# Moving second weight roundings, one output bank and one set of query loads in a thresholded attention with a squared-ReLU layer

## The chip, the cores and the metric

The kernel runs on one core of a Trainium2 chip. The metric is the device time of one execution in microseconds (us); lower is better. The core's engines work side by side, each through its own list of instructions in order: TensorE (PE) multiplies matrices, VectorE (DVE), ScalarE (ACT) and GpSimd (POOL) work on elements, and SyncE (SP) issues transfers. POOL and ACT issue transfers as well.

## The reference

For 8 batches of 8 heads with 576 rows of 64 numbers, attention whose scores below the row's maximum less `tau` are left out, then a layer with a squared ReLU over all 4608 rows:

```python
scores = np.matmul(q, k.transpose(0, 1, 3, 2)) / np.sqrt(64)
scores = np.where(scores >= max(scores, axis=-1) - tau, scores, -1e9)
attn = exp(scores - max(scores)); attn = attn / (sum(attn) + 1e-9)
x = np.matmul(attn, v)            # (B,H,S,D), turned to 4608 x 512
h = np.maximum(x @ w_in, 0.0)     # 512 x 2048
out = (h * h) @ w_out             # 2048 x 512
```

## The kernel before, in words

**Visits and steps.** Two heads of a batch are a pair; a pair is worked on in a visit `n`. A visit has steps `s`, one for each block `i` of 128 query rows; block 4 holds the last 64 rows of both heads. The first four pairs are visited twice: visits 0-3 take blocks 0 and 1 (steps 0-7), visits 4-7 blocks 2, 3, 4 (steps 8-19). Visits 8-11 take five blocks each (steps 20-39); from visit 12 on (step 40) visits go in twos, whose last 64 query rows share one step, the first of the two visits. The order of the work is written out by hand: a loop over the steps hands each engine its instructions in program order, and the engines wait for each other by semaphores alone.

**One step.** PE computes the scores into two banks (`scores`, L247); DVE takes the row maximum (L269); ACT computes the exponents (`exponents`, L277-280); DVE masks and sums (`threshold`, L292-295). There is one pair of score banks, so the next step's scores wait for the mask. POOL divides by the sum (`divide`, L300-302), for one tile of 576 columns in a step of block 4 before visit 12 and for two tiles otherwise. Two steps later PE turns the weights around (`turn`, L326-338), ACT copies them out (L327-339), and `mix` (L428) multiplies them with the values; ACT puts the result into `xT` (L411). From step 35 on (`first_dma`, visit 11) the turning is done by DVE in blocks of 32 (L366) and by transfers that SP issues (L378-391), and `mix` runs once a visit. In the last step of visits 4 to 10, DVE also turns the next visit's queries and keys (`prep`, L226) between the maximum and the mask.

**Weight roundings.** The two weight matrices come in 32 pieces `p` of 512 KB as 64-bit numbers. SP loads each into one of three areas (`load_weights`, L125), and `round_weights` rounds it in five stages: 0 two ACT copies (L137, L138), 1 and 2 three DVE operations (L140, L141, L144), 3 and 4 one POOL operation each (L146, L148). `pieces[s]` says how many are rounded in a step: one in steps 2, 4 and 6 and in each step from 8 on, but two in steps 24 and 29, up to step 34. The first of a step goes through its stages beside the step's own work. A second one gets all its stages at the step's end; on DVE that is still behind the mask and ahead of the next maximum. The end of a rounding lets SP load piece `p + 3`.

**The layer.** Rows go through the layer in chunks `j` of 256. Chunk 0 is done plainly (`j < PLAIN`): 16 calls of `mlp_in` (L476; ACT's relu L486, POOL's square L487), then 16 of `mlp_out` (L510), each of which adds the share of one of the 16 blocks of hidden units to two output banks; then ACT copies both banks to `osb` (L517) and POOL issues the store (L523). Later chunks have 16 of `mlp_in` and 14 half `product`s (L543), which read sums `gsum` that POOL makes (L466, L467) and sums of weights that DVE makes (L500). Below, each such call is a piece of the layer. `fill` hands pieces out four times in a step at a pace that `rate` sets from what is left, but only when enough roundings are done: an entry of `waiting` names the number it needs, and `usable` is the number done at the end of the step before last. Which step gets which piece is therefore fixed when the program is built. `next_bank` gives banks in turn, from 6 and 7 alone up to step 37. The plain layer's output banks are 7 for the first 128 rows and 6 for the others; the first piece of chunk 1 takes bank 6.

**Loads.** From visit 11 on queries, keys and values go into the list `loads`, which POOL works off with `some_loads`: one transfer a call, four calls a step, two a call when more than eight are in the list. `q_left` holds the last 64 query rows for a pair of visits (`load_left`, eight transfers of 8 KB, L190); DVE turns it into `qmid` (`prep_left`, L230). For visit 12 the loads are listed in step 37 behind four key loads and ahead of four query loads, and turned in step 39.

Of the kernel before, what the change touches and what calls it, by code (L numbers as in the profile page):

```python
# [19 lines left out]
def kernel(  # L20
# [10 lines left out]
    nc = tc.nc  # L31
# [3 lines left out]
    P = 128  # L35
    HP = H // 2
    NPAIR = B * HP
    NBLK = S // P
# [3 lines left out]
    NFT = d_ff // P  # L42
    TCH = 2 * P
    NCH = n_tokens // TCH
    HF, HD = NFT // 2, d_model // 2
# [17 lines left out]
    wo = const.tile([P, 7, HF, HD], FP32, name="wo")  # L63
    Q00, Q10, Q11, Q01 = range(4)
# [22 lines left out]
    q_left = const.tile([P, 2, REST // 32, 32], FP32, name="q_left")  # L87
# [68 lines left out]
    def rows_32(t, n, m):  # L156

        b, h = divmod(visits[n][0], HP)
        return t[b, 2 * h + m // 2, :, (m % 2) * 32:(m % 2) * 32 + 32].rearrange("(c p) d -> p c d", p=32)
# [21 lines left out]
    def load_left(n):  # L181

        for m in range(4):
            for v_ in range(2):
                loads.append((q_left[m * 32:(m + 1) * 32, v_, :, :], rows_32(q, n + v_, m)[:, NBLK * P // 32:, :]))

    def some_loads():
        for _ in range(min(1 + (len(loads) > 8), len(loads))):
# [85 lines left out]
    def exponents(vis, i):  # L274
        w, sc, st = weights[vis, i]
        mx, thr, bias = (st[:, j, 0:len(sc)] for j in range(3))
        nc.scalar.activation(out=bias, in_=mx, func=AF.Copy, scale=-SCALE)  # L277
        nc.scalar.activation(out=thr, in_=mx, func=AF.Identity, bias=ntau8)  # L278
        for u in range(len(sc)):
            nc.scalar.activation(out=w[:, u, :].rearrange("p (h k) -> p h k", h=2), in_=sc[u][:, :, 0:HALF],  # L280
                                 func=AF.Exp, bias=bias[:, u:u + 1], scale=SCALE)
# [220 lines left out]

    def mlp_out(j, f):

        if f == 0:
            used["o"] = [take("mm", (6, 7)) for t in range(2)]
        o = used["o"]
        for t in range(2):
            mov = wo[:, Q00:Q01 + 1:Q01 - Q00, f, :] if f < HF else wo[:, Q10:Q11 + 1, f - HF, :]
            nc.tensor.matmul(o[t].rearrange("p (h d) -> p h d", h=2), g[:, f, t * P:(t + 1) * P], mov,  # L510
                             start=(f == 0), stop=(f == NFT - 1))
        if f < NFT - 1:
            return []

        def store():
            for t in range(2):
                nc.scalar.copy(osb[:, t, :], o[t])  # L517
            store_rows(j, 0, 2)
        return [store]

    def store_rows(j, t0, t1):
        lo = j * TCH
        nc.gpsimd.dma_start(out=out[lo + t0 * P:lo + t1 * P, :].rearrange("(t p) d -> p t d", p=P), in_=osb[:, t0:t1, :])  # L523
# [57 lines left out]
    def paired(n):  # L581

        return n >= 3 * HP
# [45 lines left out]
    def pieces_of(j):  # L629

        todo = [((x // 4 + 1) * NMC, mlp_in, j, x) for x in range(NFT)]
        if j < PLAIN:
            todo += [(n_in + f + 1, mlp_out, j, f) for f in range(NFT)]
        else:
            todo += [(n_pieces, product, j, x, half) for x in range(len(PRODUCTS)) for half in range(2)]
        return todo
# [43 lines left out]
    for s, (n, i) in enumerate(steps):  # L680
        if s < HP * FIRST:
            x = int(n > 0 and i == 0)
        else:
            x = 2 if n >= 2 * HP and i == NBLK else 1
        pieces.append(min(x, left))
        left -= pieces[-1]
    assert left == 0
# [3 lines left out]
    def end_rounding(p):  # L691
        round_weights(p, 4)
        state["rounded"] += 1
        if p + RAW < n_pieces:
            load_weights(p + RAW)
# [3 lines left out]
    for s, (n, i) in enumerate(steps):  # L699
        if not by_dma(n) or i != visits[n][1][0] or paired(n) and n % 2:  # L700
            continue
        nxt = n + (2 if paired(n) else 1)
        more = nxt < len(visits)
        if paired(n):

            place_at[s + (2 if paired(n - 1) else 3)].append((n, 2, (0, 1)))
            place_at[s + 3] += [(n, 2, (2, 3)), (n, 0)]
            place_at[s + 5].append((n, 1))
            place_at[s + 8].append((n + 1, 0))
            place_at[s + 9].append((n + 1, 1))  # L710
            prep_at[s].append(lambda n=n: prep_part(q, n))
            load_at[s].append(lambda n=n: load_part(q, n + 1))
            load_at[s + 2].append(lambda n=n: load_v(n))
            prep_at[s + 4].append(lambda n=n: prep_part(q, n + 1))
            load_at[s + 4].append(lambda n=n: load_v(n + 1))
        else:
            place_at[s + 3].append((n, 0))
            place_at[s + 4].append((n, 1))
            place_at[s + 5].append((n, 2))
        if more:  # L720
            a, b, c, d = (s + 1, s + 5, s + 7, s + 8) if paired(n) else (s + 1, s + 2, s + 4, s + 4)
            load_at[a].append(lambda n=nxt: load_part(k, n))
            if paired(n):
                load_at[a].append(lambda n=nxt: load_left(n))
            prep_at[b].append(lambda n=nxt: prep_part(k, n))
            load_at[b].append(lambda n=nxt: load_part(k, n + 1))
            if not paired(n):
                load_at[b].append(lambda n=nxt: load_left(n))
            load_at[b].append(lambda n=nxt: load_part(q, n))
            prep_at[c].append(prep_left)  # L730
            prep_at[d].append(lambda n=nxt: prep_part(k, n + 1))
# [9 lines left out]
    for s in range(END + 1):  # L741
        state["step"] = s
        state["usable"] = rounded_by[-1]
        rounded_by.append(state["rounded"])
        on = s < NST
        now = []
        if on:
            n, i = steps[s]
            at = visits[n][1].index(i)
            last = at == len(visits[n][1]) - 1  # L750
            now = list(range(done, done + pieces[s]))
            done += pieces[s]
            more = n + 1 < len(visits)
            short = n < 2 * HP
            if short and at == 0 and 0 < n + 1 < 2 * HP:
                load_qk(n + 2)
            elif not short and at == 1 and not by_dma(n):
                load_qk(n + 1)
            if now:
                round_weights(now[0], 0)  # L760
            scores(s)
        old = steps[s - 2] if 2 <= s < NST + 2 and not by_dma(steps[s - 2][0]) else None
        at_once = now or old or early()
        lay = on and last and more and not by_dma(n)
        if old:
            turn(*old, 0)
            turn(*old, 1)
        if on:
            exponents(n, i)
            if at == 1:  # L770
                split_left(n)
            if lay:
                prep(n + 1)
            elif now:
                round_weights(now[0], 1)
        if s in mixes and not old:
            mix(*mixes[s])
            for j in chunk_at.get(s, ()):
                add_chunk(j)
        quarter = rate(s) / 4 if s < END else 1e9  # L780
        fill(quarter)
        if s in mixes and old:
            mix(*mixes[s])
            for j in chunk_at.get(s, ()):
                add_chunk(j)
        if old:
            turn(*old, 2)
        state["free"] = s > first_dma
        if on:
            threshold(n, i)  # L790
            for fn in prep_at[s] + load_at[s]:
                fn()
            if lay and now:
                round_weights(now[0], 1)
            if now:
                round_weights(now[0], 2)
                round_weights(now[0], 3)
            if not at_once:
                divide(n, i)
        if 0 < s <= NST and by_dma(steps[s - 1][0]):  # L800
            m, x = steps[s - 1]
            turn_blocks(m, x)
        for what in place_at[s]:
            place_blocks(*what)
        some_loads()
        fill(quarter)
        some_loads()
        if on and at_once:
            divide(n, i)
        fill(quarter)  # L810
        some_loads()
        fill(quarter)
        some_loads()
        if on:
            if now:
                end_rounding(now[0])
            for p in now[1:]:
                for stage in range(4):
                    round_weights(p, stage)
                end_rounding(p)  # L820
            if at == 0 and 0 < n <= 2 * HP:
                load_v(n)
            elif last and n >= 2 * HP and not by_dma(n):
                load_v(n + 1)
# [35 lines left out]
```

## Time and profile before

| what | value |
|---|---|
| time, median of 16 runs | 1414.88 us (1411.89 to 1416.31) |
| the profiled execution | 1415.92 us, span of its instructions 1414.1 us |
| mean granted TensorE clock | 0.989 |
| busy: PE, DVE, ACT, POOL | 1364.5, 855.7, 440.1, 922.1 us |
| eight matmuls of a layer piece, `xT` by `w_in` | 1.73 us |
| eight scores matmuls of a step | 1.17 to 1.24 us |
| one row maximum (L269), one mask (L292) | 0.75, 0.81 us |
| L140, L141, L144 at their shortest | 0.42, 0.69, 0.41 us |
| L146 and L148 on POOL | about 1.27 us each |
| POOL's issue of a `q_left` load; issue to landing | 0.55; 2.0 us |

A row of the profile names an engine, the line of the kernel, the operation, and what it writes and reads. A wait is an idle time of an engine, put down to what ended it. Times of a stretch count from the first instruction. The steps below are cut where DVE starts a step's first row maximum: step 16 at 102.5 us, 24 at 155.2, 29 at 190.6, 34 at 226.5, 37 at 255.1, 41 at 295.8.

### The profile page before, as it was taken

What the parts mean: (1) busy time and instruction counts of PE and PEld (TensorE: products, weight loads), DVE (VectorE), ACT (ScalarE), POOL (GpSimd) and SP (SyncE); (2) the same over time, 40 slices, a digit from 0 to 9 for tenths busy, and PEclk for the clock granted to TensorE, in tenths of its full rate; (3) what the DMA queues carried; (4) which work ended last, traced back from release to release, by engine and by line L of the source; (5) the groups of instructions that cost most, each with busy time, mean ns of one, the idle gap of its engine ahead of it and who ended that gap; (6) DMA issues with size and microseconds to landing.
All of it is one profiled execution on the core that took longest, in us unless ns stands there. A gap on an engine that the chain in (4) does not pass through costs nothing.

```text
span 1414.1 us, 22712 instructions
## 1 busy us (share of the span) xinstructions
PE 1364.5 (96%) x7556; PEld 1044.3 (74%) x7556; DVE 855.7 (61%) x1898; ACT 440.1 (31%) x1068; POOL 922.1 (65%) x1239
## 2 busy tenths in 40 slices
PE   5898988999999999999999999999999999999998
PEld 3676655767777777777777877777777777788887
DVE  5888887676767676766666666656666666501011
ACT  3776655222232223222222222222223222210110
POOL 3687878767777777777776858585868665422332
PEclk9999999999999999999999999999999999999999
DMA  7664531236555555554545555454445544310000
GB/s 151 133 143 107 134 99 46 51 68 130 99 116 99 114 95 110 95 107 89 104 83 112 105 109 93 100 90 96 93 103 95 120 83 95 63 42 16 1 16 15
DMA packets 397605, 127.95 MB, mean 90 GB/s; under 512 B 379952, under 2 KB 386288, under 8 KB 397488
## 3 DMA queue, kind: packets, MB, share of 16 engines
q1 hardware_dynamic: 373936, 93.01, 35.0%
q0 software_dynamic: 21168, 33.19, 8.9%
q8 instruction: 61, 1.00, 0.3%
q10 hardware_dynamic: 2384, 0.30, 0.1%
q14 instruction: 56, 0.46, 0.1%
HBM read 50.59 MB, written 9.44 MB: 42 GB/s over the span
## 4 chain that ended last, share of the span: by engine, by line
PE 87%; DVE 4%; ACT 3%; POOL 2%; issue 2%; DMA 1%; SPq 1%; POOLq 0%; ACTq 0%; DVEq 0%
PE bank L476 34%; PE bank L543 28%; PE s L247 12%; PE bank L428 10%; PE bank L326 1%; PE bank L510 1%; DVE turned L141 1%; DVE st L269 1%; ACT w L280 1%; ACT wT L327 1%; DVE w L292 1%; POOL g L487 1%; POOL w L302 0%; DVE turned L140 0%; POOL gsum L466 0%
## 5 line engine op out<-in xcount | busy, mean ns | idle before, releaser
L476 PE MATMUL bank<-xT,w_in_sb 128*128 128x256 f32 x2304 | 521.3, 384 | 2.1 <-ACT osb L517 2.1
L476 PEld LDWEIGHTS bank<-xT,w_in_sb 128*128 128x128 f32 x2304 | 433.6, 191 | 83.3 <-issue 22.3
L269 DVE TENSOR_REDUCE st<-s 128x1 f32<-128x576 f32 x288 | 205.8, 752 | 234.8 <-PE s L247 234.6
L292 DVE SCALAR_TENSOR_TENSOR w<-s,st,w 128x576 f32<-128x576 f32 x269 | 209.2, 814 | 112.3 <-ACT w L280 112.1
L543 PE MATMUL bank<-wo,gsum 128*128 128x256 f32 x1088 | 252.6, 384 | 6.1 <-POOL gsum L466 6.0
L302 POOL TENSOR_SCALAR w<-w,st 128x576 f32<-128x576 f32 x269 | 224.4, 843 | 24.8 <-DVE st L295 18.3
L543 PEld LDWEIGHTS bank<-wo,gsum 128*128 128x128 f32 x1088 | 204.0, 190 | 48.9 <-issue 12.5
L487 POOL TENSOR_TENSOR g<-g 128x512 f32<-128x512 f32 x144 | 152.0, 1056 | 114.3 <-ACT g L486 113.0
L277 ACT ACTIVATE st<-st 128x2 f32<-128x2 f32 (+1 forms) x148 | 30.3, 205 | 599.1 <-DVE st L269 598.6
L247 PE MATMUL s<-kT,qT 64*128 64x288 f32 x1024 | 175.7, 439 | 30.0 <-DVE w L292 14.8
L543 PE MATMUL bank<-wo,g 128*128 128x256 f32 x816 | 187.5, 382 | 0.0
L280 ACT ACTIVATE w<-s,st 128x576 f32<-128x576 f32 x269 | 183.3, 732 | 0.4 <-ACT st L278 0.2
L366 DVE STREAM_TRANSPOSE turned<-w 128x512 f32<-128x512 f32 (+2 forms) x388 | 168.8, 489 | 13.5 <-DMA wT<-turned 12.7
L543 PEld LDWEIGHTS bank<-wo,g 128*128 128x128 f32 x816 | 153.4, 190 | 28.4 <-issue 6.4
L428 PE MATMUL bank<-wT,vs 128*64 128x128 f32 (+7 forms) x1700 | 169.6, 359 | 3.0 <-ACT wT L327 2.6
L300 POOL TENSOR_SCALAR st<-st 128x2 f32<-128x2 f32 (+1 forms) x148 | 34.4, 232 | 207.8 <-DVE w L292 197.5
L247 PEld LDWEIGHTS s<-kT,qT 64*128 64x128 f32 x1024 | 99.1, 190 | 90.1 <-issue 61.4
L428 PEld LDWEIGHTS bank<-wT,vs 128*64 128x64 f32 (+1 forms) x1700 | 97.0, 138 | 77.3 <-issue 26.1
L486 ACT ACTIVATE g<-bank 128x512 f32<-128x512 f32 x144 | 86.1, 600 | 176.9 <-PE bank L476 175.9
L190 POOL DMA_DIRECT2D vs<-in_v_dram x144 | 90.6, 634 | 0.0
L557 DVE TENSOR_TENSOR gsum<-g 128x512 f32<-128x512 f32 x34 | 22.9, 702 | 110.6 <-PE bank L543 110.6
L146 POOL TENSOR_TENSOR turned<-turned 128x512 f32<-128x512 f32 x32 | 41.1, 1284 | 46.0 <-DVE turned L144 42.8
(73 smaller groups left out, 1049.7 us busy)
## 6 DMA issues: line engine op xcount, KB each, us to landing
wT<-turned SPq DMA_DIRECT2D x800, 72.0 KB, 2.3
out_dram<-osb POOLq DMA_DIRECT2D x34, 256.0 KB, 2.8
wo<-in_moe_w_in_dram SPq DMA_DIRECT2D x16, 512.0 KB, 4.6
wo<-in_moe_w_out_dram SPq DMA_DIRECT2D x16, 512.0 KB, 3.8
kl<-in_k_dram POOLq DMA_DIRECT2D x100, 72.0 KB, 3.1
ql<-in_q_dram POOLq DMA_DIRECT2D x100, 72.0 KB, 2.8
wT<-turned SPq DMA_DIRECT2D x192, 36.0 KB, 2.3
vs<-in_v_dram POOLq DMA_DIRECT2D x50, 128.0 KB, 3.2
```

Source lines behind the costliest of these rows:

```text
L190: nc.gpsimd.dma_start(out=to, in_=src)
L247: nc.tensor.matmul(sc[u][to, half, 0:HALF], lhsT, keys[rows, half * HALF:(half + 1) * HALF], start=True, stop=True)
L269: nc.vector.tensor_reduce(out=mx[:, u:u + 1], in_=sc[u][:, :, 0:HALF], axis=AX.XY, op=ALU.max)
L280: nc.scalar.activation(out=w[:, u, :].rearrange("p (h k) -> p h k", h=2), in_=sc[u][:, :, 0:HALF], func=AF.Exp, bias=bias[:, u:u + 1], sca ...
L292: nc.vector.scalar_tensor_tensor(out=wu, in0=sc[u][:, :, 0:HALF], scalar=thr[:, u:u + 1], in1=wu, op0=ALU.is_ge, op1=ALU.mult, accum_out=s ...
L302: nc.gpsimd.tensor_scalar(out=w[:, u, :], in0=w[:, u, :], scalar1=z[:, u:u + 1], scalar2=rcp[:, u:u + 1], op0=ALU.add, op1=ALU.mult)
L366: nc.vector.transpose(wb[:, at:at + k1 - k0, i % 2, :], w[:, u, k0 * 32:k1 * 32].rearrange("p (k q) -> p k q", q=32))
L428: nc.tensor.matmul(ps[u * D:(u + 1) * D, :], vs[n % 2][rows, u * (NBLK + 1) + c, :], wT[rows, NBLK if c == NBLK else u * (NBLK + 1) + c, a ...
L476: nc.tensor.matmul(h[:, x % 2, :], w_in_sb[:, c, f * P:(f + 1) * P], xT[:, c, at:at + TCH], start=(c == 0), stop=(c == NMC - 1))
L486: nc.scalar.activation(out=to, in_=h, func=AF.Relu)
L487: nc.gpsimd.tensor_tensor(out=to, in0=to, in1=to, op=ALU.mult)
L543: nc.tensor.matmul(to, left[:, f, :], wo[:, slot, f, :], start=(f == 0), stop=(f == HF - 1))
```

## The change

It has four parts.

1. The steps with two roundings are others. Before they were steps 24 and 29; now they are 16, 19 and 24 (block 4 of visits 6, 7 and 8). The last piece is rounded in step 33 instead of 34, and one step later than that its successors in the layer may start.
2. A second rounding's stage 0 now stands right behind the step's exponents, and stages 1 to 3 right behind the first piece's stages 2 and 3, behind the mask; only stage 4 stays at the step's end. On POOL both operations L146 so stand ahead of the step's division.
3. In the plain layer's output the last two calls change: call 14 adds blocks 14 and 15 to the first bank (7), call 15 adds both to the second (6). Each bank is copied by its own `store`; both rows are stored after the second. Call 14 now needs all 32 roundings.
4. `q_left` for visit 12 is loaded in step 27 by SP, directly, instead of in step 37 by way of `loads` and POOL.

By the planner's own working the pieces of the layer move with the gates: steps 14 to 43 had 1, 2, 1, 0, 2, 2, 0, 0, 3, 1, 1, 2, 1, 2, 1, 1, 1, 2, 1, 1, 1, 1, 5, 4, 4, 4, 4, 4, 4, 1 pieces and have 2, 1, 1, 0, 2, 2, 0, 3, 1, 1, 2, 1, 2, 1, 2, 1, 1, 1, 1, 1, 0, 5, 4, 4, 3, 4, 4, 4, 4, 1. From step 79 on both plans are the same.

```diff
 def load_left(n):
-            loads.append((q_left[...], rows_32(q, n + v_, m)[:, NBLK * P // 32:, :]))
+            what = q_left[...], rows_32(q, n + v_, m)[:, NBLK * P // 32:, :]
+            if paired(n - 1):
+                loads.append(what)
+            else:
+                nc.sync.dma_start(out=what[0], in_=what[1])
...
 def mlp_out(j, f):
-    for t in range(2):
-        mov = ... f ...
-        nc.tensor.matmul(o[t]..., g[:, f, ...], mov, start=(f == 0), stop=(f == NFT - 1))
-    if f < NFT - 1:
+    end = f - (NFT - 2)
+    for t, x in ((0, f), (1, f)) if end < 0 else ((end, NFT - 2), (end, NFT - 1)):
+        mov = ... x ...
+        nc.tensor.matmul(o[t]..., g[:, x, ...], mov, start=(x == 0), stop=(x == NFT - 1))
+    if end < 0:
         return []
     def store():
-        for t in range(2):
-            nc.scalar.copy(osb[:, t, :], o[t])
-        store_rows(j, 0, 2)
+        nc.scalar.copy(osb[:, end, :], o[end])
+        if end:
+            store_rows(j, 0, 2)
...
-            todo += [(n_in + f + 1, mlp_out, j, f) for f in range(NFT)]
+            todo += [(n_in + min(f + 1 + f // (NFT - 2), NFT), mlp_out, j, f) for f in range(NFT)]
...
-            x = 2 if n >= 2 * HP and i == NBLK else 1
+            x = 2 if HP + 2 <= n <= 2 * HP and i == NBLK else 1
...
             if not paired(n):
-                load_at[b].append(lambda n=nxt: load_left(n))
+                load_at[s - 8].append(lambda n=nxt: load_left(n))
...
             exponents(n, i)
+            for p in now[1:]:
+                round_weights(p, 0)
...
                 round_weights(now[0], 3)
+            for p in now[1:]:
+                for stage in range(1, 4):
+                    round_weights(p, stage)
...
-                end_rounding(now[0])
-            for p in now[1:]:
-                for stage in range(4):
-                    round_weights(p, stage)
+            for p in now:
                 end_rounding(p)
```

More of the change, by code (lines that the diff above doesn't have):

```diff
@@ L184, in load_left @@
             for v_ in range(2):
-                loads.append((q_left[m * 32:(m + 1) * 32, v_, :, :], rows_32(q, n + v_, m)[:, NBLK * P // 32:, :]))
+                what = q_left[m * 32:(m + 1) * 32, v_, :, :], rows_32(q, n + v_, m)[:, NBLK * P // 32:, :]
+                if paired(n - 1):
+                    loads.append(what)
+                else:
+                    nc.sync.dma_start(out=what[0], in_=what[1])
     def some_loads():
@@ L507, in mlp_out @@
         o = used["o"]
-        for t in range(2):
-            mov = wo[:, Q00:Q01 + 1:Q01 - Q00, f, :] if f < HF else wo[:, Q10:Q11 + 1, f - HF, :]
-            nc.tensor.matmul(o[t].rearrange("p (h d) -> p h d", h=2), g[:, f, t * P:(t + 1) * P], mov,
-                             start=(f == 0), stop=(f == NFT - 1))
-        if f < NFT - 1:
+        end = f - (NFT - 2)
+        for t, x in ((0, f), (1, f)) if end < 0 else ((end, NFT - 2), (end, NFT - 1)):
+            mov = wo[:, Q00:Q01 + 1:Q01 - Q00, x, :] if x < HF else wo[:, Q10:Q11 + 1, x - HF, :]
+            nc.tensor.matmul(o[t].rearrange("p (h d) -> p h d", h=2), g[:, x, t * P:(t + 1) * P], mov,
+                             start=(x == 0), stop=(x == NFT - 1))
+        if end < 0:
             return []
         def store():
-            for t in range(2):
-                nc.scalar.copy(osb[:, t, :], o[t])
-            store_rows(j, 0, 2)
+            nc.scalar.copy(osb[:, end, :], o[end])
+            if end:
+                store_rows(j, 0, 2)
         return [store]
@@ L814 @@
         if on:
-            if now:
-                end_rounding(now[0])
-            for p in now[1:]:
-                for stage in range(4):
-                    round_weights(p, stage)
+            for p in now:
                 end_rounding(p)
```

## The prediction

> **What bounds the kernel now.** I read the engine shares first, then the busy time by stretch, then the waits of TensorE, then the order of time around each wait. Columns of a stretch: its length, then busy us (instructions) of PE, PE's weight loads, DVE, ACT, POOL, then TensorE's granted clock, DMA share, GB/s.
>
> ```profile
> PE 1364.5 (96%) x7556; PEld 1044.3 (74%) x7556; DVE 855.7 (61%) x1898; ACT 440.1 (31%) x1068; POOL 922.1 (65%) x1239
> ...
> 102.51:113.53 11.02, 9.19 (x85) 6.56 (x84) 10.40 (x21) 7.69 (x19) 9.06 (x11) 1.00 0.40 112
> 155.17:170.92 15.75, 13.33 (x89) 7.33 (x88) 14.97 (x25) 9.46 (x22) 12.74 (x13) 1.00 0.53 136
> 190.57:206.05 15.48, 12.06 (x84) 7.77 (x84) 13.94 (x24) 8.88 (x21) 12.21 (x12) 0.89 0.44 124
> 255.12:295.82 40.70, 36.08 (x185) 28.53 (x185) 30.46 (x61) 10.01 (x24) 31.91 (x41) 0.96 0.42 77
> 295.82:1414.13 1118.31, 1110.32 (x5856) 866.56 (x5856) 629.31 (x1437) 279.25 (x672) 711.97 (x991) 1.00 0.44 86
> ```
>
> The stretches are cut at the first row maximum (L269) of a step: steps 16-17, 24-25, 29-30, 37-40, and 41 to the end. From step 41 on PE is idle for 8.0 us of 1118, so nothing is to be won there. Steps 24-25 and 29-30, with two roundings in their first step, keep DVE busy for 14.97 of 15.75 and 13.94 of 15.48: DVE is their bound. Steps 16-17 are held by DVE too (10.40 of 11.02). The waits of PE up to 300 us (total, times, longest):
>
> ```profile
> PE s L247 <- DVE w L292: 14.8, 11, 3.5
> PE bank L543 <- POOL gsum L466: 3.5, 1, 3.5
> PE bank L476 <- ACT osb L517: 2.1, 1, 2.1
> PE s L247 <- DVE qmid L230: 1.2, 1, 1.2
> ```
>
> The first is the mask's release of the score banks; the last three are single events of steps 36, 39 and 40. In order of time (start, us):
>
> ```profile
> 161.03 0.42 DVE L140 TENSOR_SCALAR turned<-wo 128x512 uint32<-128x512 uint32 x1
> 161.55 1.57 DVE L141 SCALAR_TENSOR_TENSOR turned<-turned 128x512 uint32<-128x512 uint32 x1
> 163.16 1.15 DVE L144 TENSOR_SCALAR turned<-turned 128x512 uint32<-128x512 uint32 x1
> 164.22 1.41 DVE L269 TENSOR_REDUCE st<-s 128x1 f32<-128x576 f32 x2
> ...
> 277.44 1.10 POOL L190 DMA_DIRECT2D q_left<-in_q_dram  x2
> 279.92 0.31 DVE L230 STREAM_TRANSPOSE qmid<-q_left 128x128 f32<-128x128 f32 x1 [3.56 <-DMA q_left<-in_q_dram]
> 290.98 3.38 PE L543 MATMUL bank<-wo,gsum 128*128 128x256 f32 x8 [3.47 <-POOL gsum L466]
> ```
>
> The second rounding of step 24 holds the next maximum back by 3.2 us. The last q_left load is issued at 277.4; DVE stands still 3.56 us for it, its next maximum is late, so ACT's exponents, the relu behind them, POOL's square and gsum are late, and PE waits 1.15 and 3.47 us.
>
> **What the Trainium skill says.** "TensorE: Matmul & The Clock Gate" (Part 1, What's actually happening): PE runs at half clock after an idle window of about 3.4 us. The trace agrees on the length (0.50 granted in 113.94:117.35, 202.69:209.51 and 291.43:294.85), but gaps of 1.3 to 3.5 us were enough. Eight matmuls then took 3.38 us instead of 1.73: a full window costs 1.7 us where PE is the bound. "GPSIMD Engine Reference" (1. Specifications): POOL shares its SBUF interfaces with VectorE and they contend when a DVE instruction has two SBUF inputs. The trace agrees: L141 takes 0.69 us alone and 1.57 beside POOL's products; L140 and L144, with one input, also stretch from 0.42 to over 1.1.
>
> **The change part by part.** Instructions are the same in number on each compute engine; eight loads go from POOL's queue to SP's. A piece costs 1.75 us of PE (8.28 us for a step with four pieces and scores, 304.09:312.37). Where pieces move, I compare for equal work: by the end of step 40 the changed kernel has done two pieces more.
>
> *Second roundings, out of 29 and into 16 and 19 (24 keeps two; 34 has none).* Step 16: DVE runs without a gap from its maximum to the next, so the added L140+L141+L144 lie on the path: 0.42+0.69+0.43 = 1.5 alone, 3.2 as in step 24. With step 17's own L140/L141 beside POOL's products, I take **+3.2** (1.5 to 4.6). Step 19: DVE waits 1.45 us there before the next maximum, so 3.2-1.45 plus 0.25 for the neighbour: **+2.0** (0 to 3.5). Step 21 then has three pieces right after the idle of step 20, where the half-clock window of 134.42 fell on steps without pieces: **+1.2** (0 to 1.7). Steps 29-31 (24.32 us, four pieces; then three): the second rounding 2.4, the contended part of step 30's first (0.95+1.56 against 0.42+0.69) 1.4, and two half-clock windows that reach into step 31 (8.84 us for a content of 7.5) 1.3: **-5.1** (-6.5 to -3).
>
> *The order within a doubled step.* Stage 0 of the second piece is now on ACT ahead of the copies and relu (two instructions, 0.68 each; ACT is busy 9.46 of 15.75). On POOL both products L146 stand before the division L302: the division of a single-tile step (1.1 us) is one product, 1.3 us, plus its wait for DVE later. Queued behind it: both L148 and the next step's L146. PE needs that division two steps later, at the transposes: cover about 2.8 us in step 18, more in step 26. DVE's order is unchanged, but L144 and the next L140 get clear of POOL's square and late L146: steps 24-25 **-0.7** (-1.5 to +0.5).
>
> *The plain layer's end.* Pieces 14 and 15 now each finish one bank; piece 14 must wait for the last rounded weight, so step 34 has none and 35 has five. Step 34 loses its rounding and falls from 7.14 to 5.0. Step 35: scores, transposes and mix 4.0, five pieces 8.75. The next layer's first piece takes the bank that ends last (bank 6); its copy (0.54) stands on ACT behind mix's copy and the turn's, so PE waits 1.3 where it waited 2.1, plus half a slow window 0.9. Step 36: 4.0 and four pieces, 11. Sum 30.95 for nine pieces against 28.58 for seven and 3.5 for two more: **-1.1** (-3 to +3).
>
> *q_left by SP in step 27.* POOL issues eight loads less (0.55 each, 4.4 us, from steps 37-39); behind them k and q loads, squares and gsum move up. The 3.56 us wait of DVE goes; the key load behind it landed long before. SP issues eight more ahead of the weight load of step 27, 0.59 each by its v loads: 4.7 us late, but used three steps (some 17 us) on; landing of 512 KB takes 4.6. Hidden; without that cover ACT would wait up to 4.7. Late next is PE itself: steps 37-40 become four steps of 8.28 plus mix 0.95 and 0.75 of small waits = 34.8 against 40.70: **-5.9** (-6.5 to -3). In steps 43 and 61 a layer now starts right behind its mix; step 79 does so already with no wait shown, so 0 (to +0.5 each).
>
> Sum: 3.2+2.0+1.2-5.1-0.7-1.1-5.9 = **-6.4**. The profiled execution took 1415.92 (span 1414.1), 1.0 above the median of the 16 runs: 1409.5 on its scale, **1408.5** on the median's.
>
> **Rivals.** *Early roundings covered*: if both take the uncontended 1.5, with DVE's 1.45 hiding step 19's, 1.7 fall away at step 16, 2.0 at 19 and with its idle the 1.2 at 21: 1403.6. For: steps 18 and 19 are at PE's limit. Against: DVE's 10.40 of 11.02. *The wait moves on*: behind q_left DVE meets the next late load (ql, kl), and -5.9 shrinks to -0.5: 1413.9. For: single waits for ql of 1.3 us; against: those loads move up as well. *POOL's division late* (slower): POOL is in order; if it runs more than the 2.8 us of cover behind, PE's transposes wait in steps 18, 21 and 26 for a division behind two products: 2.5 us (product and wait), then a slow window of 1.7, three times 4.2 = 12.6: 1421.1. For: POOL is busy 17.43 of 20 us in 100:120, and visits 6 and 7 get two products, 2.6 us, more each. Against: it is busy for only 7.11 of 12.60 us in steps 19-20. *The change does not do what it says* (the bank that ends first is not the one wanted next): that is so already in my sum, which gives that part only 0.5 of wait.
>
> **How the numbers follow.** Likeliest 0.48: 1408.5, own range 1404.5 to 1412.5. Early roundings covered 0.15, wait moves on 0.16, POOL late 0.21. About 0.2%, 2.8 us, is what a measurement of this kernel can tell from no change: faster is below 1412.1, slower above 1417.7. Faster 0.45+0.15+0.02 = 0.62; same 0.03+0.13+0.02 = 0.18; slower 0.20. Range 1402 to 1419: it leaves out the upper part of the POOL case and the best ends of the first.
>
> **What would show it.** Right: no DVE wait for q_left; PE's waits for gsum in step 40 and for qmid gone; granted clock 1.00 at 285-300; steps 29-30 near 12 us; steps 16-17 near 14 and 19-20 near 14.6; PE waiting about 1.3 for osb. Wrong: PE waiting for POOL's w (L302) at transposes; ACT waiting for a weight load near step 30; PE idle after 300 above 8 us; steps 37-40 still above 37 us.

## The result, and the profile after

The changed kernel takes 1410.83 us (median of 9 runs, 1409.55 to 1412.06) beside 1415.24 for the kernel before (48 runs): a ratio of 0.9969, 95% interval 0.9962 to 0.9977, or 4.4 us less. The prediction was 1408.5, 6.4 less. The profiled execution took 1411.41 us, span 1409.6, against a span of 1414.1 before. Lines of the changed kernel stand 4 to 6 further down (L247 is now L251, L269 L273, L292 L296, L466 L470, L500 L504, L517 L522, L543 L549; L137 to L148 stay).

From the page, the engine shares; under it, from the view of stretches, steps 16-17, 19-20, 24-25, 29-30 and 37-40, cut at the first maximum of a step as before (columns as in the prediction):

```profile
PE 1361.5 (97%) x7556; PEld 1042.2 (74%) x7556; DVE 856.5 (61%) x1898; ACT 440.4 (31%) x1068; POOL 917.5 (65%) x1231
```

```profile
103.11:117.83 14.72, 9.79 (x84) 6.99 (x84) 13.30 (x24) 9.24 (x22) 12.04 (x12) 0.93 0.46 133
127.29:140.59 13.30, 11.16 (x92) 8.19 (x92) 12.29 (x24) 9.33 (x22) 9.66 (x9) 0.97 0.44 130
163.00:176.14 13.14, 12.90 (x89) 7.40 (x88) 12.39 (x24) 8.89 (x21) 10.03 (x12) 1.00 0.50 143
196.49:208.48 11.99, 11.36 (x85) 6.77 (x84) 10.58 (x21) 8.06 (x19) 6.22 (x8) 1.00 0.42 116
258.49:296.79 38.30, 34.27 (x182) 27.19 (x183) 36.42 (x62) 9.20 (x23) 25.95 (x33) 1.00 0.43 81
```

The total work has hardly moved (PE 3.0 us less). Steps 16-17 are dearer, 24-25 and 29-30 cheaper. In the last line DVE is busy for 36.42 of 38.30 us, where it was 30.46 of 40.70: that is where the largest expected gain went.

The waits of PE up to 300 us in the changed kernel (total, times, longest), without those of the start:

```profile
PE s L251 <- DVE w L296: 14.7, 10, 3.8
...
PE s L251 <- DVE qT L230: 2.6, 1, 2.6
PE bank L480 <- ACT osb L522: 1.1, 1, 1.1
...
PE s L251 <- DVE qmid L234: 0.4, 1, 0.4
```

The wait of 3.5 for POOL's `gsum` is gone, and the one for `qmid` has shrunk to 0.4; a wait of 2.6 for `qT`, the turned queries of step 41, is new.

All stretches for equal work (a layer piece more or less counted at 1.75 us, steps 37 to 42 with 24 pieces before and 23 after):

| steps | before, us | after, us | difference for equal work | predicted |
|---|---|---|---|---|
| 16-17 | 11.02 | 14.72 | +3.7 | +3.2 |
| 18 | 8.65 | 9.46 | +0.8 | 0 |
| 19-20 | 12.61 | 13.30 | +0.7 | +2.0 |
| 21-23 (one piece more) | 20.38 | 22.41 | +0.3 | +1.2 |
| 24-25 | 15.75 | 13.14 | -2.6 | -0.7 |
| 26-28 (one more) | 19.65 | 20.35 | -1.05 | 0 |
| 29-31 (one less) | 24.32 | 17.41 | -5.2 | -5.1 |
| 32-33 | 11.65 | 12.28 | +0.6 | 0 |
| 34-36 (two more) | 28.58 | 32.32 | +0.2 | -1.1 |
| 37-42 (one less) | 57.25 | 53.60 | -1.9 | -5.9 |
| 43 to the end (two less) | 1101.7 | 1097.5 | -0.7 | 0 |

With 0.6 by which step 16 starts later, the differences add up to -4.6; the spans differ by 4.5. The prediction cut its -5.9 at step 41. There the stretch is 40.70 against 38.30 with one piece less, only -0.65: the changed kernel's step 41 begins behind a wait of PE and is then shorter (7.31 against 8.27), so I cut at step 43, where both run alike.

### The profile page after: what moved, and what is told of

Its sections match the earlier page's. It is cut to its first block, busy times and chain, and to the rows that moved or that the text cites. A ratio compares the mean times of both kernels' runs of the same rounds, so it can differ in the third digit from the quotient of the medians.

```text
span 1409.6 us, 22706 instructions
## 1 busy us (share of the span) xinstructions
PE 1361.5 (97%) x7556; PEld 1042.2 (74%) x7556; DVE 856.5 (61%) x1898; ACT 440.4 (31%) x1068; POOL 917.5 (65%) x1231
## 4 chain that ended last, share of the span: by engine, by line
PE 87%; DVE 4%; ACT 3%; POOL 2%; issue 2%; DMA 1%; SPq 1%; POOLq 0%; ACTq 0%; DVEq 0%
PE bank L480 34%; PE bank L549 28%; PE s L251 12%; PE bank L432 10%; PE bank L516 2%; PE bank L330 1%; ACT wT L331 1%; DVE wo L504 1%; DVE st L273 1%; ACT w L284 1%; DVE w L296 1%; DVE turned L141 1%; POOL kl L194 0%; POOL w L306 0%; POOL g L491 0%
## 5 line engine op out<-in xcount | busy, mean ns | idle before, releaser
L273 DVE TENSOR_REDUCE st<-s 128x1 f32<-128x576 f32 x288 | 205.7, 752 | 231.6 <-PE s L251 231.4
L296 DVE SCALAR_TENSOR_TENSOR w<-s,st,w 128x576 f32<-128x576 f32 x269 | 209.2, 814 | 110.7 <-ACT w L284 110.4
L549 PE MATMUL bank<-wo,gsum 128*128 128x256 f32 x1088 | 248.9, 382 | 2.2 <-POOL gsum L470 2.1
L306 POOL TENSOR_SCALAR w<-w,st 128x576 f32<-128x576 f32 x269 | 223.9, 841 | 25.4 <-DVE st L299 19.2
L549 PEld LDWEIGHTS bank<-wo,gsum 128*128 128x128 f32 x1088 | 203.9, 190 | 41.3 <-issue 9.8
L251 PE MATMUL s<-kT,qT 64*128 64x288 f32 x1024 | 176.8, 442 | 32.3 <-DVE w L296 13.9
L549 PE MATMUL bank<-wo,g 128*128 128x256 f32 x816 | 188.3, 382 | 0.0
L549 PEld LDWEIGHTS bank<-wo,g 128*128 128x128 f32 x816 | 153.0, 190 | 30.0 <-issue 8.7
L251 PEld LDWEIGHTS s<-kT,qT 64*128 64x128 f32 x1024 | 99.6, 191 | 92.6 <-issue 64.9
L194 POOL DMA_DIRECT2D kl<-in_k_dram x100 | 68.9, 693 | 0.0
```

What stands on the lines that cost most here:

```text
L194: nc.gpsimd.dma_start(out=to, in_=src)
L251: nc.tensor.matmul(sc[u][to, half, 0:HALF], lhsT, keys[rows, half * HALF:(half + 1) * HALF], start=True, stop=True)
L273: nc.vector.tensor_reduce(out=mx[:, u:u + 1], in_=sc[u][:, :, 0:HALF], axis=AX.XY, op=ALU.max)
L296: nc.vector.scalar_tensor_tensor(out=wu, in0=sc[u][:, :, 0:HALF], scalar=thr[:, u:u + 1], in1=wu, op0=ALU.is_ge, op1=ALU.mult, accum_out=s ...
L306: nc.gpsimd.tensor_scalar(out=w[:, u, :], in0=w[:, u, :], scalar1=z[:, u:u + 1], scalar2=rcp[:, u:u + 1], op0=ALU.add, op1=ALU.mult)
L549: nc.tensor.matmul(to, left[:, f, :], wo[:, slot, f, :], start=(f == 0), stop=(f == HF - 1))
```

## What holds steps 37 to 40 now

From the order of time in the changed kernel, step 37 and steps 39-40 (start, us, engine, line, operation):

```profile
265.06 5.34 DVE L504 TENSOR_TENSOR wo<-wo 128x512 f32<-128x512 f32 x3
...
266.56 1.61 POOL L470 TENSOR_TENSOR gsum<-g 128x512 f32<-128x512 f32 x1
...
268.25 1.60 POOL L471 TENSOR_TENSOR gsum<-gsum,g 128x512 f32<-128x512 f32 x1
...
281.88 0.31 DVE L234 STREAM_TRANSPOSE qmid<-q_left 128x128 f32<-128x128 f32 x1
...
284.23 4.72 DVE L504 TENSOR_TENSOR wo<-wo 128x512 f32<-128x512 f32 x4
...
284.53 1.59 POOL L470 TENSOR_TENSOR gsum<-g 128x512 f32<-128x512 f32 x1
286.20 1.60 POOL L471 TENSOR_TENSOR gsum<-gsum,g 128x512 f32<-128x512 f32 x1
288.88 1.41 DVE L273 TENSOR_REDUCE st<-s 128x1 f32<-128x576 f32 x2
```

`qmid` is turned at 281.88 with no idle time ahead of it: the wait for `q_left` is gone, as the change intends. But next in DVE's queue now stand the sums of weights (L504), which read two SBUF inputs. In step 37 three of them take 5.34 us beside a square and two `gsum` operations of POOL, 1.78 each; in step 39 four take 4.72, 1.18 each; one alone takes 0.68. The next maximum at 288.88 waits for them. Before, the groups of three took 2.88, 3.05 and 2.70; two lines of that trace:

```profile
261.70 2.88 DVE L500 TENSOR_TENSOR wo<-wo 128x512 f32<-128x512 f32 x3
...
273.98 0.68 DVE L500 TENSOR_TENSOR wo<-wo 128x512 f32<-128x512 f32 x1
```

This is the contention that the prediction took from the Trainium skill ("GPSIMD Engine Reference", 1. Specifications) for L141; the trace agrees for L504 too, and I had not applied it there. "SBUF — State Buffer" (SBUF: two separate sides) calls the shared port pair an exclusive lock, so that one of the two waits for the other's whole instruction. The first group fits that: three sums at 0.68, POOL's square at 1.05 and two `gsum` operations at 1.27 (what one takes in e1 below with no sum beside it) make 5.6 us one after another, and DVE took 5.34. For the second group the same working gives 5.3 and is too high, since only two of its four sums are held up. The instructions one by one show it best. The second sum of the first group is this row:

```profile
266.97 1.75 DVE L504 TENSOR_TENSOR wo<-wo 128x512 f32<-128x512 f32 x1
```

It ends at 268.72, which is 0.55 us after the end of the `gsum` operation that began at 266.56. In the changed kernel up to 300 us, each of the eight sums that take over 0.9 us ends 0.54 to 0.56 us after a POOL instruction that it overlaps, and so do all twelve L141 of that length. A sum that has to wait thus costs what is left of the POOL instruction, and some 0.55 us more.

That gave me two theories to test. P: each part is worth what the prediction says, and the profile's stretches only scatter. S: `q_left` is worth less, because the sums on DVE hold up the same steps. For the steps before, the rivals were on the order within a doubled step (O: it is worth much more than 0.7, since it also frees the following step) and on moving the roundings (D: they are better one double later).

## The experiments

Each was timed in five rounds beside the kernel before on the same chip. A ratio is to the kernel before; 0.001 is 1.4 us. The kernels ran in three groups, on three chips, and the changed kernel itself was timed apart from them; differences between two ratios are therefore uncertain by about 1.5 us.

### `q_left` alone (e1) and the change without it (e2)

e1 is the kernel before with only the `load_left` part of the diff; e2 is the changed kernel with

```diff
-                load_at[s - 8].append(lambda n=nxt: load_left(n))
+                load_at[b].append(lambda n=nxt: load_left(n))
```

and the loads in the list again.

> The kernel before with the early q_left load by SP alone. Theory P (the prediction's sum): DVE's 3.56 us wait for q_left goes and with it PE's waits of 1.15 and 3.47 us and a half-clock window: -5.9 us, about 1409. Theory S (DVE's sums of weights, L500, beside POOL's gsum take the place of the wait, but only where the layer's pieces stand three ahead, as in the changed kernel): the pieces have not moved here, so most of it is gained too, -3.5 to -5.5. Theory N (the wait only moves to another load): within 1 us of before.

> The changed kernel with q_left loaded by POOL from the list again, all else kept. Theory P: 5.9 us slower than the changed kernel, 1416.7. Theory S: q_left's gain was taken by the sums in steps 37 to 40, so only 0 to 2.5 us slower than the changed kernel, 1411 to 1413.3.

e1: 0.998 (0.9972 to 0.9988), -2.8 us. e2: 0.9997 (0.9989 to 1.0005), so taking `q_left` out of the changed kernel gives back 4.0 us. Neither is the 5.9 of P; S expected too little of e2 and slightly too much of e1. The order of time in e1 shows what remains:

```profile
276.92 0.31 DVE L234 STREAM_TRANSPOSE qmid<-q_left 128x128 f32<-128x128 f32 x1
...
287.99 3.61 PE L547 MATMUL bank<-wo,gsum 128*128 128x256 f32 x8 [2.55 <-POOL gsum L470]
```

DVE no longer waits for `q_left`, step 39 falls from 11.57 to 8.03 us, and yet PE still waits 2.55 of its 3.47 us for `gsum` in step 40. That wait had not hung on `q_left` alone, as the prediction's chain (q_left, maximum, exponents, relu, gsum) had it.

### The sums a step earlier (e3)

```diff
-        state["free"] = s > first_dma
+        state["free"] = s >= first_dma
```

DVE may begin the sums in step 35, before POOL has any `gsum` to make.

> The changed kernel with the sums of weights allowed from step 35 instead of 36, so that the three pieces of the next layer in step 35 take one sum each, when DVE has been idle for 9.9 us. Theory P (the sums are not the bound): same as the changed kernel, 1410.8 within 0.7. Theory S: three sums fewer in steps 37 to 40 at 1.2 to 1.8 us each, PE's wait of 2.64 in step 40 gone: 2 to 4 us faster than the changed kernel, 1407 to 1409.

0.9955 (0.9942 to 0.9967), -6.4 us: some 2 us better than the changed kernel. The intervals of the two just overlap; the profile has the same size. Step 39 falls from 10.08 to 7.81, step 40 from 7.92 to 7.32, and step 43 starts 2.2 us earlier counted from step 28. In its order of time, the sums of steps 35, 37 and 39:

```profile
238.66 1.27 DVE L504 TENSOR_TENSOR wo<-wo 128x512 f32<-128x512 f32 x2
...
265.45 5.35 DVE L504 TENSOR_TENSOR wo<-wo 128x512 f32<-128x512 f32 x3
...
284.64 2.45 DVE L504 TENSOR_TENSOR wo<-wo 128x512 f32<-128x512 f32 x2
```

Two sums were made in step 35 at 0.64 us each, and in step 39 two stand where four stood: 2.45 us instead of 4.72. PE's idle time in step 40 falls from 2.64 to 0.37. So that wait was the sums', as S said.

### The order within a doubled step: alone (e4) and undone (e7)

e4 is the kernel before with the last three hunks of the diff (stages 0 to 3 of the second piece moved forward); e7 is the changed kernel without them.

> The kernel before with the second rounding's stages put behind the exponents and the mask, in its two doubled steps 24 and 29, and nothing else. Theory P: -0.7 for each, -1.4, 1413.5. Theory O (what steps 24-25 won in the changed kernel, 15.75 to 13.15 us, comes of the order): about -2.5 each, -5, 1410. Theory M (steps 24-25 won by the pieces of the layer that moved, not by the order): 0, 1415.

> The changed kernel with all stages of a second rounding at the step's end again. Theory P: 3 doubles at 0.7 each, 2.1 us slower, 1413. Theory O (as the order alone did, 4.4 us for two doubles): 4 to 7 us slower than the changed kernel, 1415 to 1418, and in the trace L141 beside POOL's L146 and L148 in the step after each double.

e4: 0.9977 (0.9963 to 0.999), -3.3 us. e7: 0.9995 (0.9985 to 1.0006), 3.7 us slower than the changed kernel. The prediction has 0.7 a double from step 24: 1.4 for e4's two doubles and 2.1 for e7's three. The order is worth about twice that; each run alone leaves the prediction's figure at the edge of its uncertainty, the two together speak against it. In e4 steps 24-25 fall from 15.75 to 13.99 and 29-30 from 15.48 to 14.16, 3.1 us together. In e7 the steps behind a double are 7.13, 7.14 and 6.38 us long (17, 20, 25), against 5.58, 5.31 and 5.00 in the changed kernel. The order of time in the changed kernel says why; DVE first, then POOL, from the end of step 24:

```profile
168.67 0.42 DVE L140 TENSOR_SCALAR turned<-wo 128x512 uint32<-128x512 uint32 x1
169.19 1.57 DVE L141 SCALAR_TENSOR_TENSOR turned<-turned 128x512 uint32<-128x512 uint32 x1
170.80 0.43 DVE L144 TENSOR_SCALAR turned<-turned 128x512 uint32<-128x512 uint32 x1
...
172.47 0.45 DVE L140 TENSOR_SCALAR turned<-wo 128x512 uint32<-128x512 uint32 x1
173.02 0.69 DVE L141 SCALAR_TENSOR_TENSOR turned<-turned 128x512 uint32<-128x512 uint32 x1
```

```profile
171.37 1.27 POOL L146 TENSOR_TENSOR turned<-turned 128x512 f32<-128x512 f32 x1 [1.15 <-DVE turned L144]
...
173.11 1.31 POOL L306 TENSOR_SCALAR w<-w,st 128x576 f32<-128x576 f32 x1
174.38 2.70 POOL L148 TENSOR_TENSOR wo<-turned 128x512 f32<-128x512 f32 x2
```

Within the step only L144 gets shorter (0.43 where it was 1.15): that is the 0.7. But with both L146 ahead of the division, the two L148 (2.70 us) begin only at 174.38, when the next step's L140 and L141 on DVE are over; these take 0.45 and 0.69. Before, step 25's L140 fell beside L148 and its L141 beside the second piece's late L146, and they took 1.28 and 1.57; from that trace, DVE and then POOL:

```profile
165.56 1.28 DVE L140 TENSOR_SCALAR turned<-wo 128x512 uint32<-128x512 uint32 x1
166.94 1.57 DVE L141 SCALAR_TENSOR_TENSOR turned<-turned 128x512 uint32<-128x512 uint32 x1
...
165.28 1.27 POOL L148 TENSOR_TENSOR wo<-turned 128x512 f32<-128x512 f32 x1
166.51 1.45 POOL L146 TENSOR_TENSOR turned<-turned 128x512 f32<-128x512 f32 x1
```

I had named L144 and the next L140 as the ones that get clear, and left the next L141 out.

### The doubled steps: moved alone (e9), put back (e5)

```diff
-            x = 2 if n >= 2 * HP and i == NBLK else 1
+            x = 2 if HP + 2 <= n <= 2 * HP and i == NBLK else 1
```

is e9's one edit to the kernel before; e5 undoes it in the changed kernel.

> The kernel before with the doubled steps moved to 16, 19 and 24 and nothing else: all stages of a second rounding still at the step's end. Theory P (the prediction's sum for this part): +1.3 us, 1416. Theory O (in the old order the first step after each double pays for POOL's L146 and L148 beside L141, and three doubles pay more than two): +2 to +4, 1417 to 1419. Theory G (the layer's pieces that come sooner pay for it): -1 to -2, 1413.

> The changed kernel with the two roundings of steps 24 and 29 again (and the last in step 34), the order within a doubled step, the bank end and the early q_left kept. Theory P (moving the doubles costs 1.3 by the prediction's sum, new ones +6.4, old one -5.1): 1.3 us faster than the changed kernel, 1409.5. Theory D (in the new order an old double costs only some 2.5, so the move costs more, 3 to 4): 1407 to 1408. Theory K (the move pays): slower than the changed kernel, over 1412.

e9: 1.0031 (1.0019 to 1.0044): 4.4 us slower than before, which fits O (2 to 4) and not P (1.3). e5: 0.9976 (0.9967 to 0.9986), in 22 runs from 1408.4 to 1417.6; against the changed kernel's 0.9969 the intervals overlap, so the move is worth from a loss of about 1 to a gain of about 3 there. P (e5 faster than the changed kernel by 1.3) is at the edge of that, D (3 to 4 faster) outside it. The two together show that the parts do not add up: alone, in the old order and with the old gate, the move costs 4.4; within the change no loss shows. e9's profile shows three places: steps 16-17 take 16.33 us, 19-20 14.73 (with idle PE in 17 and 20 of 4.84 and 2.92), and step 39, with `q_left` still late, 13.87 us with 4.59 of it idle.

### The end of the plain layer: undone (e6), and its gate alone (e10)

e6 has both banks end in the last call and the old numbers of roundings again; e10 puts back the call only and keeps the changed gate:

```diff
-        end = f - (NFT - 2)
-        for t, x in ((0, f), (1, f)) if end < 0 else ((end, NFT - 2), (end, NFT - 1)):
+        for t in range(2):
...
             todo += [(n_in + min(f + 1 + f // (NFT - 2), NFT), mlp_out, j, f) for f in range(NFT)]
```

> The changed kernel with both output banks ended in the last call again and the old gates. Step 34 gets a piece of the layer again. Theory P: the bank end is worth 0.5 of wait in it, with the empty step against it: within 1 us of the changed kernel. Theory E (the empty step 34, 2.8 us of PE idle and a half-clock window after it, costs more than the bank end saves): 1 to 3 us faster than the changed kernel.

> The changed kernel with both output banks ended in the last call, but with the new gate (call 14 waits for all 32 roundings, so no piece of the layer stands in step 34). The version with the old end and the old gate was 4.4 us slower than the changed kernel. Theory Gate (there the piece in step 34 waited 2.1 us for POOL's L148 and shifted the sums of weights beside POOL's gsum): about the changed kernel plus 0.5 us, 1411.3. Theory Bank (the early copy of one bank is what pays): 4 us slower than the changed kernel, 1415.

e6: 0.9999 (0.9991 to 1.0006), 4.2 us slower than the changed kernel; neither P (about nothing) nor the rival that it is faster holds. e10: 0.9971 (0.9961 to 0.9981), the same as the changed kernel. So of this part the gate pays. Of the early bank the traces show 0.5 us, by which PE waits longer in e10's step 35 (idle 1.55 against 1.05); the timed runs can't tell that from nothing. In e6 PE, DVE and PE again, in order of time:

```profile
229.41 2.50 PE L515 MATMUL bank<-wo,g 128*128 128x512 f32 x4 [2.07 <-POOL wo L148]
...
278.37 5.07 DVE L504 TENSOR_TENSOR wo<-wo 128x512 f32<-128x512 f32 x3
...
286.92 1.77 PE L251 MATMUL s<-kT,qmid 64*64 64x288 f32 x16 [2.79 <-DVE qmid L234]
```

With the old gate a piece stands in step 34 and waits 2.07 us for the last rounding on POOL; and since the layer is then a piece further at the end of step 38, another group of sums falls there beside two squares and four load issues of POOL (5.07 us for three sums, with no `gsum` in that time) and holds `qmid` up, for which PE waits 2.79. For equal work, e6 against e10: step 34 +0.8 (9.32 against 6.61, less 1.88 for the piece), step 37 +1.75 (the same 11.83 us for three pieces as for four), steps 38-40 +2.3 (30.56 against 26.49 with a piece less), 4.9 of the 5.2 by which the profiled spans differ.

### Later doubles with early sums (e8)

```diff
-            x = 2 if HP + 2 <= n <= 2 * HP and i == NBLK else 1
+            x = 2 if HP + 3 <= n <= 2 * HP + 1 and i == NBLK else 1
```

on top of e3: doubles in 19, 24 and 29 instead of 16, 19 and 24.

> The changed kernel with doubles in steps 19, 24 and 29 instead of 16, 19 and 24, and the sums of weights from step 35 on. Step 16-17 falls back from 14.7 to 11.0, steps 29-30 rise from 12.0 to some 14.2. Against the version with the sums alone (1407.5): Theory D (a double costs less where its step holds more else, and step 16 is the worst place): 1 to 2 us faster, 1406. Theory Z (a double costs the same anywhere): same, 1407.5 within 1.

0.9934 (0.9919 to 0.9948), -9.3 us, median 1405.01: the lowest ratio of the kernels that compute everything as the reference does. Its upper end lies below the changed kernel's interval; against e3 (0.9955) the intervals overlap. In the profile steps 16-17 take about what they took before the change (11.7), while 29-30 take 13.0, not 15.48: with the new order a double in 29 is much cheaper than the one that the change took away.

### Six sums at once (e11), and visit 11's loads by SP (e12)

```diff
+            if s == first_dma:
+                some_sums(6)
```

behind the mask of step 35 and two sums a piece in step 36 is e11 on top of e8's doubles. e12 is e11 with the queries and keys of visit 11 loaded by SP ahead of time (`if by_dma(n)` becomes `if paired(n)`). It loads the second head's keys of that visit with their rows turned by 64, so that head's part of the output is another one; its time is read only for what the wait in step 34 costs.

> The version with doubles in steps 19, 24 and 29, but six sums of weights at once in step 35, behind its mask, where DVE had been idle, and two instead of one per piece in step 36. Theory S (DVE's sums beside POOL's gsum bound steps 37 to 40): step 37 falls from 11.8 to under 10 and PE's last waits before step 41 go: 1 to 2.5 us faster than with three sums in step 35 (1405.0), 1403 to 1404. Theory P (three were enough, PE is the bound again): 1405 within 0.7.

> As the version with six sums, and the queries and keys of visit 11 loaded by SP at once in step 31 instead of by POOL from the list. In the changed kernel DVE waits 2.3 us for ql in step 34 and PE is idle 2.8 us in it. Theory L (that wait goes as q_left's did, with a half-clock window after it): 2 to 3.5 us faster than the version with six sums. Theory M (the rounding and POOL hold step 34 anyway): within 0.7 of it.

e11: 0.9942 (0.9926 to 0.9959), not to be told from e8. In its profile steps 38, 39 and 40 take 5.83, 6.94 and 8.53 us with 0.8 us of idle PE in all, and 37 to 42 together 49.7 with 23 pieces: for equal work 5.8 less than before (57.25 with 24), which is what the prediction wanted of `q_left`. So PE is what comes next there, once the sums are out of the way. The median does not show it against e8, and the profiled run is the fastest of six. What spreads e11's runs is the granted clock: 1400.04 us at a mean of 0.998, 1402.48 at 0.996, 1405.05 at 0.994, and three of 1408.71 to 1408.87 at 0.991. From 0.998 to 0.991 is 0.7% of 1400 us, an estimated 9.8 us, and the times differ by 8.8. e12: 0.9905 (0.9892 to 0.9918), four runs. The wait that it takes away is this one, in the changed kernel's step 34, from the order of time:

```profile
229.23 0.78 DVE L230 STREAM_TRANSPOSE qT<-ql 128x576 f32<-128x576 f32 x1 [2.30 <-DMA ql<-in_q_dram]
```

Step 34 falls from 5.61 in e11 to 4.37 in e12, PE's idle time in it from 1.81 to 0.57. Those 1.2 us are shown. The two ratios differ by some 5 us, the spans of the two profiles hardly at all (1398.3 and 1398.7). The median granted clock is 0.9925 in e11's runs and 0.9955 in e12's, which by the same estimate is worth some 4 us; whether the edit or chance made that difference, no run shows.

## Why the prediction was right or wrong

The sign and the range were right: 1410.83 lies within 1402 to 1419 and within the likeliest case's own 1404.5 to 1412.5. The sum was right within 2 us by errors that offset each other, and that it came so near is luck.

- **Second roundings.** 29-31 was right (-5.2 against -5.1; steps 29-30 are 11.99, "near 12"). 16-17 was nearly right (+3.7, of it the second L141 at 1.57), but its stall reaches into step 18 (+0.8): PE's idle time of 4.93 us there is followed by 6.8 us at half clock. Steps 19-20 gained over the estimate (+0.7 against +2.0) and step 21 too (+0.3 against +1.2). These terms, with step 18, add up to +0.3, where the prediction had +1.3. Step 20 is 5.31 us long, against 7.14 in e7, so what the prediction overcharged there is the order's effect on the step after a double. The rival that early roundings are covered did not happen at step 16. Steps 26-28, priced at nothing, are 1.05 better; a stretch at half clock that began at 172.0 before is not there.
- **The order within a doubled step** was mis-sized: -0.7 in the sum, -2.6 in steps 24-25 and 3.7 by experiment over all three doubles. The failed step is the sentence that only L144 and the next L140 get clear of POOL. The slower rival, POOL's division late, did not happen: PE waits for L306 nowhere in the list of its waits up to 300 us.
- **The plain layer's end.** The waits were right (1.05 us for `osb` where 1.3 was named). Step 34 was not: 7.22 us instead of 5.0. DVE waits 2.30 us for a `ql` load there, the line shown above, of which e12 gives back 1.2. The -1.1 became +0.2, with a stretch at half clock from 232.0 in it: e2, which does the same work there without one, has steps 34 and 35 shorter by 0.5 and 1.0. What I priced was the early bank; what pays in this part is the gate, 4.0 us between e6 and e10, because of what the layer meets in steps 34 and 38 to 40.
- **`q_left` by SP** was the largest error: -5.9 in the sum, -1.9 in the stretch, and 2.8 to 4.0 by e1 and e2. The load is hidden on SP (its eight issues take 4.33 us, where I used 4.7) and DVE's wait of 3.56 is gone. The failed step is "late next is PE itself": late next were DVE's own sums, which take 1.2 to 1.8 us each on average beside POOL's squares and `gsum`, and steps 37-40 stayed at 38.3, above the 37 named as wrong. It was the only sign of being wrong that came: PE waits for no division, ACT for no weight load near step 30, and PE is idle for 7.4 us after 300. The rival "the wait moves on" was right in kind, and wrong in what it named: not a load but contention.

What stays open: why the parts' effects do not add up. Taken out singly, the four are worth 4.0, 3.7, about 1 and 4.2 us, 12.9 together, where the whole change is worth 4.4; three of them put in alone are worth 2.8, 3.3 and -4.4. In part the pieces of the layer and the sums move with each of them, as e6 shows; the rest is not shown. The plain layer's end alone on the kernel before was not tried.

## What to carry to other kernels

When a wait is taken away, list what stands behind it on the same engine and price that work beside what the neighbouring engines will then be doing; here two-input sums at 0.68 us came to as much as 1.78 each and ate the gain. Judge a reordering by the step after it as well: moving one POOL operation (the second L146) ahead of a division paid most in the following step. And test parts both alone and by removal, since a move that cost 4.4 us alone showed no loss within the change.

## What the runs showed of the hardware that I had not expected

- The Trainium skill ("TensorE: Matmul & The Clock Gate", Part 1, What's actually happening) says that the idle window of about 3.4 us is free-running, so that warming up at a kernel's start differs from run to run. Here this holds in the middle of the work as well. The lengths agree (3.4 or 6.8 us in every trace up to 300 us). Within a trace they begin whole multiples of 3.413 us apart (before: 28.61, 113.94 and 134.42, 25 and 6 of them), from an offset that differs between traces (1.3 us before, 3.3 in the changed kernel). A window need not be idle throughout: in these two traces, from 50 to 300 us, PE is idle for 1.1 to 3.2 of the 3.41 us ahead of each such stretch, while some windows with up to 1.8 us of idle are followed by none. And where such stretches lie differs between kernels with the same work: up to step 24 e4 does what the kernel before does, whose trace has stretches at 28.6, 113.9 and 134.4, and e4's has none before 197.9. So a few us between two profiles can be theirs, and a difference of one stretch is read from the timed rounds rather than from the trace.
- DVE operations with one input stretch beside POOL as well: L140 takes 0.42 to 0.45 us alone and 1.19 to 1.24 in steps 16 and 24, where it meets POOL's square and L148. All 13 L140 and L144 that take over 0.7 us in the changed kernel up to 300 us end 0.28 to 0.31 us after a POOL instruction that they overlap, so they wait as the sums do. "GPSIMD Engine Reference" (1. Specifications) names DVE's 2-port performance modes beside two SBUF inputs as what contends; whether L140 runs in such a mode, no run here shows.
